# When the turned y is moved, cast and multiplied: the loads of the MLP's input in two chunks of a mixer kernel, and a third tile of w1's products ahead

## The chip, the cores and the metric

The kernel runs on one core of one Trainium2 chip. The metric is the device time of one execution in microseconds (us); the median of several executions is what is compared. A difference of about 0.3% can be told from no change.

## The reference, cut to what matters

One sequence of S = 2048 tokens of width D = 512. Two branches read the same layer-normalised input and their results are multiplied:

```python
xn = layernorm(x)
s = attention(xn, wqkv, wo)      # 32 heads of 16, causal, window of 256 tokens
y = layernorm(xn)
h = gelu(y @ w1 + b1)            # 512 -> 1792
g = silu(h @ w2 + b2)            # 1792 -> 512
out = x + s * g
```

All is float32. The kernel makes a float32 product from three products of two halves: a high part, which is a cast to the matmul's type fp32r, and a low part, which is the value less its high part (`PASSES`).

## The kernel before, in words

**Stages.** First x is normalised and turned. Then comes attention, written as 128 steps, t = 0 to 127 (`end = 16 * NQ`), from 16 starting steps on: each step has the scores and softmax of one block of 128 keys for four heads (`prob_block`, step t), the row maxima of a block 12 steps ahead (`max_block`, m = t + 12), the products with v (`pv_step`), and fills. Fills are matmuls of other work that keep TensorE (PE) busy: the projections of q and k of later heads and of v, and, from step 99 on, the first products with w1 of the first chunk of 512 tokens (`pair_h`). `tandem(t0, t1, one, two)` spreads a pair of such jobs over the slots of steps t0 to t1 and copies the two banks `fb` out at t1. `at(t, ...)` puts an operation into the middle of step t, `behind(t, ...)` at its end.

After attention follow the chunks of 512 tokens, one after another. The loop `for c in range(2)` does the first (c = 0) and the second (c = 1). In its step i it applies the gelu to tile `order[i]` of the 14 tiles of hidden features (`activate`: gelu and cast `gh` on ScalarE, the low part `gl` on VectorE), multiplies tile `order[i - 1]` with w2 (`project`, 12 matmuls), and makes the products of tile `order[i + 2]` with w1 (`hidden`, 12 matmuls) unless attention made them already. `end_chunk` adds b2, applies the silu, multiplies the attention output with wo (banks `s`, two at a time) and gates (`gated<-s,gated` on VectorE). Chunks 2 and 3 are done together afterwards with combined operands; their inputs (`first_y`, `second_y`, `combine_w`) are prepared in the steps of c = 1.

**What y is and how it is turned.** w1's products need y with features on the partitions, so y must be turned. Two ways are used. For the first chunk 16 PE transposes through the banks `fb` do it (`y_turn`, in steps 91 and 92 of attention). For the others VectorE turns 32 x 32 blocks in place (`turn_y`), the tile is written to DRAM (`z_d`), and four transfers for each group of 128 features fetch it in the turned order in pieces of 128 bytes (`fetch_y`, 16 transfers a chunk). `settle_y` then makes the high part (cast on ScalarE) and the low part (subtraction on VectorE) of one such group. The steps of the layer norm itself are the list `mlp["ln"]`, run piecewise by `y_steps(a, b)`: four statistics, one inversion, one shift, four normalisations.

**Where the second chunk's y stands before.** In c = 0: loaded at i = 4, statistics at i = 6 and 7, normalised at i = 10 and 11, turned at i = 11 and 12, fetched at i = 13 (all 16 transfers). It is settled inside `end_chunk(0)`, by `between(0)` and `between(2)`, ahead of the gating of the same places.

**What sets the order.** Each engine works its instructions in the order in which the program has them. SyncE (SP), which issues all transfers, keeps program order until the end of attention; behind that, its order is the one that the scheduler gives. PSUM pools hold the banks: in the chunk stage `ps_st` has two banks (w1's products and `s`), `ps_yt` two, which nothing uses until chunks 2 and 3, and `ps_mx` the accumulators `acc`.

Of the kernel before, what the change touches and what calls it, by code (L numbers as in the profile page):

```python
# [18 lines left out]
P = 128  # L19
# [31 lines left out]
def mixer_kernel(ctx, tc, x, wqk, wv, wo, w1, b1, w2, b2, out):  # L51
# [311 lines left out]
    def pair_qk(n, c):  # L363
# [11 lines left out]
        def finish(ps, t, copy):  # L375
# [383 lines left out]
    at(99, open_w1)  # L759
    for f, t in ((6, 91), (7, 91), (8, 92), (9, 94), (10, 94), (11, 99), (12, 99), (13, 101), (2, 101), (3, 103), (0, 103),  # L760
                 (1, 105), (4, 105), (5, 107)):
        at(t, fetch, "w1", f)
    for f, t, lo_at, lo_by in ((6, 94, 95, nc.vector), (7, 95, 97, on_pool), (8, 96, 98, on_pool), (9, 97, 99, nc.vector),
                               (10, 100, 102, nc.vector), (11, 102, 103, nc.vector), (12, 103, 105, on_pool),
                               (13, 105, 106, on_pool), (2, 106, 108, nc.vector), (3, 107, 109, on_pool),
                               (0, 108, 110, on_pool), (1, 109, 112, nc.vector), (4, 111, 113, on_pool),
                               (5, 112, 114, on_pool)):
        at(t, settle, "w1", f, nc.scalar.copy)
        at(lo_at, settle, "w1", f, None, lo_by)
# [101 lines left out]

    for g in range(4):
        fetch("wo", g)

    def load_y(c):
# [3 lines left out]

    def turn_y(c, i):  # L880

        y = mlp["y"][i]
        nc.vector.transpose(y, y)
        nc.sync.dma_start(z_d[c, i], y)

    def fetch_y(c, kt, dst):

        for k in range(4):
            at = z_d[c, 0, 0, 128 * kt + 32 * k: 128 * kt + 32 * k + 32]
            nc.sync.dma_start(dst[32 * k: 32 * k + 32].rearrange("p (t j) -> p t j", j=32),  # L890
                              bass.AP(tensor=at.tensor, offset=at.offset, ap=[[512, 32], [32 * 512, 16], [1, 32]]))

    def settle_y(kt):

        hi, lo = mlp["yy"][0][kt], mlp["yy"][1][kt]
        split(hi, lo, lo.bitcast(F32))

# [159 lines left out]
    def steps2(i):  # L1057

        if i in (-1, 1, 5, 6):
            mlp["ln"] = layernorm(mlp["y"], f"C{2 + (i > 1)}_{i}", True)  # L1060
            y_steps(0, 2 if i < 0 else 5)
        if i == 0:
            y_steps(2, 5)

    gated = None
    for c in range(2):
# [18 lines left out]
        order = [2, 3, 0, 1, 4, 5, *range(6, NF)] if c == 0 else [*range(NF)]  # L1085
        if c:
            hidden(0)
            hidden(1)
        o_from, o_late = (0, 0) if c else (8, 1)
        for i in range(NF + 1):  # L1090
            if i < NF:
                activate(order[i])
            if c and i in (1, 2, 6, 7):
# [11 lines left out]
            if i >= 1:  # L1105
                project(accs, [(order[i - 1], gs.pop(order[i - 1]))], order[0], order[-1])
            if i + 2 < NF and order[i + 2] not in made and order[i + 2] > 1:
                hidden(order[i + 2])
            if c == 0:
                if i == 2:  # L1110
                    den = fetch_sums()
                if 4 <= i < 8:
                    nc.vector.reciprocal(den[:, P * (i - 4): P * (i - 3)], den[:, P * (i - 4): P * (i - 3)])
                    if i == 7:
                        nc.sync.dma_start(rden_d.rearrange("g a (c t) -> (g a c) t", c=NCH), den)
                if i == 4:
                    mlp["y"] = load_y(1)
                if i == 6:
                    mlp["ln"] = layernorm(mlp["y"], "C1", False)
                for back, (a, b) in enumerate(((0, 2), (2, 4), (4, 5), (5, 6), (6, 8), (8, 10))):  # L1120
                    if i == 6 + min(back, 5):
                        y_steps(a, b)
                if i in (11, 12):
                    turn_y(1, 2 * i - 22)
                    turn_y(1, 2 * i - 21)
                if i == 13:
                    for kt in range(KT):
                        fetch_y(1, kt, mlp["yy"][1][kt].bitcast(F32))
                    mlp["y"] = load_y(2)
            else:  # L1130
                steps2(i)
                if i == 3:
                    for k in range(4):
                        turn_y(2, k)
                if i == 4:
                    kept[0] = gated[:, 2:4]
                    kept[1] = bigp.tile([P, 2, 512], F32, tag="wb1", name="y2_21")
                    for kt in range(KT):
                        fetch_y(2, kt, kept[kt // 2][:, kt % 2])
                    mlp["y"] = load_y(3)  # L1140
                if i in (5, 6):
                    first_y(2 * i - 10)
                    first_y(2 * i - 9)
# [15 lines left out]
            if 0 <= k < 4:  # L1159
                wanted.append(load_o(c, k))  # L1160
            if c and i in (0, 1, 5, 6):
                y_steps(5, 6)
# [161 lines left out]
```

## Time and profile before

| | |
|---|---|
| median of 3 runs | 758.77 us (757.1 to 759.68) |
| the profiled execution's own time | 758.06 us |
| its span, first to last instruction | 756.3 us |
| PE busy | 732.9 us (97%) |
| VectorE (DVE) busy | 517.6 us (68%) |
| ScalarE (ACT) busy | 438.4 us (58%) |
| GpSimd (POOL) busy | 298.7 us (39%) |
| DMA packets | 84025, of them 36640 under 512 bytes |

Times are counted from the span's start. Attention's steps end at about 431 us, c = 0 runs to about 495 us, c = 1 to about 587 us, chunks 2 and 3 to the end. PE matmuls overlap each other, so that the step between their starts is shorter than one's duration. In a row of the timeline, what stands in brackets is the engine's idle time before the row, and what ended it. All of the kernel's instructions are recorded under one helper's line (L43), so rows are told apart by the names of the tiles: `xnT`, `yh` are areas that hold y's halves in the chunk stage, `w` and `wos` hold w2's and wo's, `or` and `ohl` are the attention output before and behind its split, `w<-rden_d` brings in the reciprocals of the softmax sums.

### The profile page before, as it was taken

Reading aid. Unit: us, or ns where it says so; the run is one execution under the profiler, and the core shown is the slowest. Engines: PE = TensorE matmul, PEld = TensorE weight load, DVE = VectorE, ACT = ScalarE, POOL = GpSimd, SP = SyncE. Lnnn points to the kernel's source line nnn. Section 1 sums busy time; section 2 is a strip of 40 time slices with the busy share of each in tenths; the row PEclk is TensorE's granted clock in tenths of the full one; section 3 lists DMA queues with packets and bytes.
Section 4 is the critical chain, followed back from the end, with each engine's and each line's share of the span. In section 5 each row is a group of like instructions: output and inputs, shape, how many; then the busy total and the mean of one; then the engine's idle time right before and its main releaser. Section 6 shows DMA issues by size and latency. Waiting matters only on the chain.

```text
span 756.3 us, 18805 instructions
## 1 busy us (share of the span) xinstructions
PE 732.9 (97%) x7360; PEld 587.3 (78%) x7360; DVE 517.6 (68%) x793; ACT 438.4 (58%) x740; POOL 298.7 (39%) x644
## 2 busy tenths in 40 slices
PE   8999999999999999999999999799999999999997
PEld 7886777777778887776776787588778888888886
DVE  7886777877766779887873458656558765676643
ACT  7757767867676676788867645244534643442001
POOL 7414767766666555859776400030101100001102
PEclk9999999999999999999999999899999999999999
DMA  8633346766655544646634474857253232244621
GB/s 292 183 77 81 87 120 160 215 160 164 162 137 137 144 120 127 169 119 178 196 107 135 144 251 129 202 158 183 53 139 98 98 107 72 73 161 131 204 61 56
DMA packets 84025, 105.71 MB, mean 140 GB/s; under 512 B 36640, under 2 KB 36896, under 8 KB 83936
## 3 DMA queue, kind: packets, MB, share of 16 engines
q1 hardware_dynamic: 83936, 104.50, 49.5%
q8 instruction: 58, 0.95, 0.5%
q14 instruction: 31, 0.25, 0.1%
HBM read 54.53 MB, written 32.77 MB: 115 GB/s over the span
## 4 chain that ended last, share of the span: by engine, by line
PE 80%; DVE 6%; ACT 5%; DMA 3%; issue 2%; POOL 1%; SPq 1%; DVEq 0%; ACTq 0%; POOLq 0%
PE fb L43 18%; PE acc L43 15%; PE zo L43 11%; PE p L43 9%; PE stb L43 9%; PE s L43 6%; PE xy L43 5%; PE h L43 4%; ACT pt L43 4%; PE pv L43 3%; SPq L43 1%; POOL pt L43 1%; DVE y L43 1%; DVE xy L43 1%; DMA w<-rden_d 1%
## 5 line engine op out<-in xcount | busy, mean ns | idle before, releaser
L43 POOL TENSOR_SCALAR_AFFINE_SELECT pt<-pt 128x256 f32<-128x256 f32 x480 | 192.9, 426 | 133.7 <-ACT pt L43 131.7
L43 ACT ACTIVATE pt<-stb 128x768 f32<-128x768 f32 (+1 forms) x244 | 188.5, 773 | 62.5 <-PE stb L43 55.0
L43 DVE TENSOR_REDUCE mt<-xy 128x4 f32<-128x1024 f32 (+1 forms) x128 | 152.6, 1192 | 4.4
L43 DVE COPY_PREDICATED xy<-upper,zo 128x512 f32<-128x512 int32 x112 | 77.8, 695 | 70.5 <-PE xy L43 62.9
L43 POOL TENSOR_TENSOR xo<-xo,gated 128x512 f32<-128x512 f32 x15 | 19.9, 1331 | 225.2 <-DVE gated L43 218.1
L43 PE MATMUL fb<-xnT,wqb 64*128 64x512 f32 (+1 forms) x684 | 104.6, 397 | 0.2
L43 PE MATMUL zo<-pt,vt 128*17 128x128 f32 x2880 | 103.8, 275 | 0.3 <-POOL pt L43 0.3
L43 PE MATMUL stb<-qk 64*128 64x384 f32 (+1 forms) x488 | 97.1, 393 | 6.1 <-ACT pt L43 3.9
L43 PE MATMUL acc<-w,gh 128*128 128x512 f32 x320 | 98.6, 389 | 0.0
L43 PEld LDWEIGHTS stb<-qk 64*128 64x128 f32 x488 | 45.9, 183 | 51.4 <-ACT pt L43 46.2
L43 PEld LDWEIGHTS zo<-pt,vt 128*17 128x17 f32 x2880 | 67.5, 97 | 15.6 <-issue 6.4
L43 PEld LDWEIGHTS fb<-xnT,wqb 64*128 64x128 f32 (+1 forms) x684 | 64.6, 185 | 11.0 <-DVE pjr L43 1.4
L43 PEld LDWEIGHTS acc<-w,gh 128*128 128x128 f32 x320 | 60.1, 188 | 12.4
L43 PE MATMUL acc<-w,gl 128*128 128x512 f32 x160 | 62.8, 392 | 0.9 <-DVE gl L43 0.9
L43 PE MATMUL xy<-qk 64*128 64x256 f32 (+2 forms) x536 | 58.4, 291 | 0.2 <-DVE mt L43 0.2
L43 PEld LDWEIGHTS xy<-qk 64*128 64x128 f32 x536 | 46.7, 185 | 6.7 <-issue 3.1
L43 PE MATMUL s<-wos,ohl 128*128 128x512 f32 (+1 forms) x204 | 47.2, 392 | 4.7 <-DVE gated L43 4.7
L43 ACT COPY oraw<-zo 128x128 f32<-128x128 f32 x128 | 34.0, 266 | 29.3 <-PE zo L43 28.8
L43 PEld LDWEIGHTS s<-wos,ohl 128*128 128x128 f32 x204 | 38.6, 198 | 12.8 <-DVE gated L43 5.1
L43 ACT ACTIVATE gated<-acc 128x512 f32<-128x512 f32 x16 | 8.7, 595 | 64.3 <-DVE acc L43 64.3
L43 PEld LDWEIGHTS zo<-qk 64*128 64x128 f32 x448 | 38.3, 185 | 4.6 <-issue 1.4
L43 ACT COPY p<-p 128x512 f32<-128x512 f32 x21 | 12.3, 585 | 47.4 <-PE p L43 40.1
(188 smaller groups left out, 1234.0 us busy)
## 6 DMA issues: line engine op xcount, KB each, us to landing
qk<-sh SPq DMA_DIRECT2D x128, 128.0 KB
qk<-pjr SPq DMA_DIRECT2D x64, 128.0 KB
oT_d<-oraw SPq DMA_DIRECT2D x32, 256.0 KB
w_d<-in_w_dram SPq DMA_DIRECT2D x14, 512.0 KB
x<-in_x_dram SPq DMA_DIRECT2D x16, 256.0 KB
or<-oT_d SPq DMA_DIRECT2D x16, 256.0 KB
w<-rden_d SPq DMA_DIRECT2D x16, 256.0 KB
xo<-in_x_dram SPq DMA_DIRECT2D x16, 256.0 KB
```

The costliest lines, as they stand in the source:

```text
L43: r = issue(*args, **kwargs)
```

## The change

It has five parts.

1. The first chunk's y is no longer turned by PE. VectorE turns it (at the ends of steps 83, 85, 86 and 87), four transfers write it and 16 fetch it, two in each of steps 88 to 95; it is settled in steps 93 to 100, half a group in each. The layer norm's pieces run one to two steps earlier. The fills of the last group of heads go over steps 85 to 91 and 92 to 98 (before 85 to 90 and 93 to 98), and w1's first tiles are fetched and split some steps later; one low part goes from GpSimd to VectorE.
2. The second chunk's y is loaded at the start of the chunk stage, ahead of wo, normalised in steps i = 2 to 6 of c = 0, and turned at i = 6 and 7. Its 16 fetches are spread over i = 8 to 13 and its casts over i = 11 to 14 of the loop; `between` no longer holds them.
3. wo is fetched at i = 2.
4. In c = 1, w1's products are made three tiles ahead instead of two; the odd tiles take the banks of `ps_yt`, so four banks are used.
5. What c = 1 does for chunks 2 and 3 (second layer norm of the last chunk, `first_y`, `second_y` and what follows them) stands one step later, with the first chunk-2 transfers over two steps.

```diff
-            free += 2 * (t == 90)
...
-    def y_turn(kt):
-        for i in range(4):
-            nc.tensor.transpose(fb[kt % 2][:, P * i: P * (i + 1)], mlp["y"][i][:, P * kt: P * (kt + 1)], ident)
-        split(mlp["yy"][0][kt], mlp["yy"][1][kt], fb[kt % 2])
+    def turn_y(c, i):
+        y = mlp["y"][i]
+        nc.vector.transpose(y, y)
+        return z_d[c, i], y
+
+    def fetch_y(c, kt, dst, groups=range(4)):
+        for k in groups:
+            at = z_d[c, 0, 0, 128 * kt + 32 * k: 128 * kt + 32 * k + 32]
+            nc.sync.dma_start(dst[32 * k: 32 * k + 32].rearrange("p (t j) -> p t j", j=32),
+                              bass.AP(tensor=at.tensor, offset=at.offset, ap=[[512, 32], [32 * 512, 16], [1, 32]]))
+
+    def settle_y(kt, part=None, src=None):
+        hi, lo = mlp["yy"][0][kt], mlp["yy"][1][kt]
+        halves(hi, lo, lo.bitcast(F32) if src is None else src, part)
...
-                               ((75, 79), (80, 84)), ((85, 90), (93, 98))), 2):
+                               ((75, 79), (80, 84)), ((85, 91), (92, 98))), 2):
...
-    for i, t in enumerate((77, 78, 81, 82, 83, 83, 85, 86, 87, 89)):
+    for i, t in enumerate((76, 77, 78, 81, 82, 82, 83, 85, 86, 87)):
         at(t, y_steps, i, i + 1)
+        if i >= 6:
+            at(t, lambda i=i, t=t: behind(t, nc.sync.dma_start, *turn_y(0, i - 6)))
     at(88, open_yy)
-    for kt in range(KT):
-        fills.setdefault((91 + kt // 2, kt % 2), []).append((y_turn, (kt,)))
+    for m in range(4 * KT):
+        at(88 + m // 2, lambda kt=m // 4, k=m % 4: fetch_y(0, kt, mlp["y"][kt], (k,)))
+    for kt, t in enumerate((93, 95, 98, 99)):
+        for part in range(2):
+            at(t + part, lambda kt=kt, part=part: settle_y(kt, part, mlp["y"][kt]))
...
-    for f, t in ((6, 91), (7, 91), (8, 92), (9, 94), (10, 94), ...
+    for f, t in ((6, 93), (7, 94), (8, 96), (9, 96), (10, 97), ...
...
-    for g in range(4):
-        fetch("wo", g)
...
+    mlp["y"] = load_y(1)
...
-        if i in (-1, 1, 5, 6):
+        if i in (-1, 1, 6, 7):
             mlp["ln"] = layernorm(mlp["y"], f"C{2 + (i > 1)}_{i}", True)
...
-            hs[f] = ps_st.tile([P, 512], F32, tag="b", name=f"h_{c}_{f}")
+            hs[f] = (ps_yt if c and f % 2 else ps_st).tile([P, 512], F32, tag="b", name=f"h_{c}_{f}")
...
-        if c:
-            hidden(0)
-            hidden(1)
+        ahead = 2 + c
+        for f in range(ahead if c else 0):
+            hidden(f)
...
-            if c and i in (10, 12):
+            if c and i in (11, 13):
                 rest[0]()
-            if c and i in (10, 13):
+            if c and i in (11, 13):
                 rest[1]()
...
-            if i + 2 < NF and order[i + 2] not in made and order[i + 2] > 1:
-                hidden(order[i + 2])
+            if i + ahead < NF and order[i + ahead] not in made and order[i + ahead] > 1:
+                hidden(order[i + ahead])
...
-                if i == 4:
-                    mlp["y"] = load_y(1)
-                if i == 6:
+                if i == 2:
+                    for g in range(4):
+                        fetch("wo", g)
                     mlp["ln"] = layernorm(mlp["y"], "C1", False)
-                for back, (a, b) in enumerate(((0, 2), (2, 4), (4, 5), (5, 6), (6, 8), (8, 10))):
-                    if i == 6 + min(back, 5):
-                        y_steps(a, b)
-                if i in (11, 12):
-                    turn_y(1, 2 * i - 22)
-                    turn_y(1, 2 * i - 21)
-                if i == 13:
-                    for kt in range(KT):
-                        fetch_y(1, kt, mlp["yy"][1][kt].bitcast(F32))
+                if 2 <= i < 7:
+                    y_steps(2 * i - 4, 2 * i - 2)
+                if i in (6, 7):
+                    for k in (2 * i - 12, 2 * i - 11):
+                        nc.sync.dma_start(*turn_y(1, k))
+                for m in range(max(0, 3 * i - 25), min(16, 3 * i - 22)) if i >= 8 else ():
+                    fetch_y(1, m // 4, mlp["yy"][1][m // 4].bitcast(F32), (m % 4,))
+                if i >= 11:
+                    settle_y(i - 11)
+                if i == 14:
                     mlp["y"] = load_y(2)
...
-                if i == 8:
+                if i == 9:
                     for k in range(4):
-                        turn_y(3, k)
+                        nc.sync.dma_start(*turn_y(3, k))
                     fetch_second(0)
-                if i in (9, 11):
-                    rest = second_y(i // 11)
-                if i == 10:
+                if i in (10, 12):
+                    rest = second_y(i // 12)
+                if i == 11:
                     fetch_second(1)
...
         def between(i):
-            if c == 0 and i in (0, 2):
-                settle_y(i)
-                settle_y(i + 1)
```

More of the change, by code (lines that the diff above doesn't have):

```diff
@@ L759, in mixer_kernel @@
     at(99, open_w1)
-    for f, t in ((6, 91), (7, 91), (8, 92), (9, 94), (10, 94), (11, 99), (12, 99), (13, 101), (2, 101), (3, 103), (0, 103),
+    for f, t in ((6, 93), (7, 94), (8, 96), (9, 96), (10, 97), (11, 99), (12, 99), (13, 101), (2, 101), (3, 103), (0, 103),
                  (1, 105), (4, 105), (5, 107)):
         at(t, fetch, "w1", f)
-    for f, t, lo_at, lo_by in ((6, 94, 95, nc.vector), (7, 95, 97, on_pool), (8, 96, 98, on_pool), (9, 97, 99, nc.vector),
-                               (10, 100, 102, nc.vector), (11, 102, 103, nc.vector), (12, 103, 105, on_pool),
+    for f, t, lo_at, lo_by in ((6, 96, 97, nc.vector), (7, 97, 98, nc.vector), (8, 100, 102, on_pool), (9, 101, 104, nc.vector),
+                               (10, 104, 106, nc.vector), (11, 102, 103, nc.vector), (12, 103, 105, on_pool),
                                (13, 105, 106, on_pool), (2, 106, 108, nc.vector), (3, 107, 109, on_pool),
@@ L878, in load_y @@
         return [load(mlp["yp"], "y", xn_d[4 * c + i], f"y_{c}_{i}") for i in range(4)]
[L880 to L896, printed above, removed]
+    mlp["y"] = load_y(1)
     def fetch_sums():
@@ L1092, in mixer_kernel @@
                 activate(order[i])
-            if c and i in (1, 2, 6, 7):
+            if c and i in (1, 2, 7, 8):
                 y_steps(6, 10)
-            if c and i in (10, 12):
+            if c and i in (11, 13):
                 rest[0]()
-            if c and i in (10, 13):
+            if c and i in (11, 13):
                 rest[1]()
@@ L1133, in mixer_kernel @@
                     for k in range(4):
-                        turn_y(2, k)
+                        nc.sync.dma_start(*turn_y(2, k))
                 if i == 4:
@@ L1137, in mixer_kernel @@
                     kept[1] = bigp.tile([P, 2, 512], F32, tag="wb1", name="y2_21")
-                    for kt in range(KT):
+                if i in (4, 5):
+                    for kt in (2 * i - 8, 2 * i - 7):
                         fetch_y(2, kt, kept[kt // 2][:, kt % 2])
+                if i == 5:
                     mlp["y"] = load_y(3)
-                if i in (5, 6):
-                    first_y(2 * i - 10)
-                    first_y(2 * i - 9)
-                if i == 8:
+                for kt in {6: (0, 1), 7: (2,), 8: (3,)}.get(i, ()):
+                    first_y(kt)
+                if i == 9:
                     for k in range(4):
-                        turn_y(3, k)
+                        nc.sync.dma_start(*turn_y(3, k))
                     fetch_second(0)
-                if i in (9, 11):
-                    rest = second_y(i // 11)
-                if i == 10:
+                if i in (10, 12):
+                    rest = second_y(i // 12)
+                if i == 11:
                     fetch_second(1)
@@ L1160, in mixer_kernel @@
                 wanted.append(load_o(c, k))
-            if c and i in (0, 1, 5, 6):
+            if c and i in (0, 1, 6, 7):
                 y_steps(5, 6)
```

## The prediction, made before the changed kernel was run

> **What bounds the kernel now.** I read the page first, for the engine that fills the span.
>
> ```profile
> span 756.3 us, 18805 instructions
> ...
> PE 732.9 (97%) x7360; PEld 587.3 (78%) x7360; DVE 517.6 (68%) x793; ACT 438.4 (58%) x740; POOL 298.7 (39%) x644
> ```
>
> PE leaves 23.4 us of the span. A change pays if it takes work off PE, fills its gaps, or keeps its clock up. So I next asked for windows by stage (columns: length, then busy time of PE, PEld, DVE, ACT, POOL, then granted clock, DMA share, GB/s), and for what PE waited for in the chunk stage.
>
> ```profile
> 432.20:477.20 45.00, 44.11 (x193) 35.63 (x192) 31.35 (x56) 22.88 (x37) 1.39 (x1) 1.00 0.58 193
> 477.20:495.70 18.50, 13.79 (x50) 10.87 (x49) 7.87 (x12) 5.93 (x9) 2.41 (x2) 0.82 0.88 218
> 495.70:580.80 85.10, 81.86 (x359) 66.88 (x358) 53.43 (x106) 40.07 (x63) 8.00 (x7) 1.00 0.46 119
> ```
> ```profile
> PE s L43 <- DVE gated L43: 4.7, 1, 4.7
> PE h L43 <- ACT g L43: 3.2, 2, 1.8
> PE acc L43 <- DVE gl L43: 0.9, 2, 0.5
> ```
>
> The middle window, the end of the first chunk, is the only one in which PE both waits long and runs at a clock below 1. The timeline there shows the chain.
>
> ```profile
> 471.41 1.30 DVE L43 STREAM_TRANSPOSE y<-y 128x512 f32<-128x512 f32 x2
> ...
> 475.94 0.86 SPq L43 DMA_DIRECT2D z_d<-y  x2
> ...
> 477.40 5.60 PE L43 MATMUL s<-wos,ohl 128*128 128x512 f32 x24
> ...
> 479.89 8.78 SPq L43 DMA_DIRECT2D xnT<-z_d  x16
> ...
> 483.97 0.62 ACT L43 CAST yh<-xnT 128x512 fp32r<-128x512 f32 x1 [2.37 <-DMA xnT<-z_d]
> 484.62 0.69 DVE L43 TENSOR_TENSOR xnT<-xnT,yh 128x512 fp32r<-128x512 f32 x1 [4.14 <-ACT yh L43]
> ...
> 486.97 1.28 DVE L43 TENSOR_TENSOR gated<-s,gated 128x512 f32<-128x512 f32 x2
> 487.71 8.34 PE L43 MATMUL s<-wos,ohl 128*128 128x512 f32 x24 [4.71 <-DVE gated L43]
> ...
> 495.88 0.39 PE L43 MATMUL h<-yh,xnT 128*128 128x512 f32 x1
> ```
>
> The second chunk's y is turned late, written at 475.94 and fetched from 479.89. VectorE's queue has the low halves of that y ahead of the gating, so the gating of the first `s` bank, whose matmuls had long ended, waits for a transfer; `s` has two banks, so PE stands for 4.71 us. Then 24 matmuls take 8.34 us where the same 24 took 5.60. That 2.74 us is the clock's, by the 0.82 of the window. The gap and its echo cost 7.45 us.
>
> The Trainium skill (TensorE: Matmul & The Clock Gate, part 1 on the clock gate) says that about 3.4 us without work drop PE to half clock until it has been busy for as long. The 4.71 us gap and the window's 0.82 agree.
>
> **The change part by part: the end of the first chunk.** y goes through the same stations five steps earlier, and its casts stand inside the loop. The 4.71, the 2.74 and the two stalls on `gl` (0.9, which the turning at i = 11 and 12 caused) go: 8.35 us. What is late next? PE works one `project` in 12 x 44.11 / 193 = 2.74 us, and VectorE now has more than that in i = 5 to 7.
>
> ```profile
> 450.38 0.94 DVE L43 RECIPROCAL den<-den 128x128 f32<-128x128 f32 x1
> ...
> 463.59 1.00 DVE L43 TENSOR_SCALAR y<-y,mvC,rsC 128x512 f32<-128x512 f32 x2
> ```
>
> With 0.69 for a low half (row 484.62), i = 5 has `gl`, a low half of w2, a reciprocal and two normalisations: 3.32 us. i = 6 has two turns (1.30, row 471.41) on top, 4.62; i = 7 the same without normalisations, 3.62. The excess over 2.74 is 0.58 + 1.88 + 0.88 = 3.34 us. `gh` has two buffers, so `gl` of a tile can start only when PE begins the tile before it, and it is needed at the third matmul of its own, 2 x 0.23 = 0.46 us in: of 2.74 + 0.46, the cast takes 0.62 and the low half 0.69, which leaves 1.9 us of slack. So PE loses 3.34 - 1.9 = 1.4 us (none if VectorE enters i = 5 early, 2.4 if it enters a microsecond late, since y's load now precedes the sums' on SP). Queued behind this on VectorE is the reciprocal whose write SP needs before `w<-rden_d`, and SP now has the fetches between those loads: eight fetches at 8.78 / 16 = 0.55 us stand ahead of the third. The product with `or` waits, and `gl` behind it: I take 0.9 us, with bounds 0 and 1.5. The last cast comes about a microsecond before the gating needs VectorE, so I expect no hole. Net: -8.35 + 1.4 + 0.9 = -6.05 us, between -8.35 and -4.45. wo's later fetch is hidden: it takes the place that y's load had on SP, and wo's first split was and stays at i = 6.
>
> **Attention.** PE loses 16 transposes; VectorE gets four turns and SP 20 transfers.
>
> ```profile
> L43 DVE STREAM_TRANSPOSE y<-y x12: 668/670/708, 468.0 to 549.4; 128x512 f32<-128x512 f32 x12
> ```
> ```profile
> 326.93 0.45 PE L43 MATMUL stb<-qk 64*128 64x384 f32 x2 [0.17 <-ACT pt L43]
> 327.31 0.66 PE L43 MATMUL fb<-ident,y 128*128 128x128 f32 x4
> 327.89 0.44 PE L43 MATMUL zo<-qk 64*128 64x128 f32 x4
> ...
> 346.30 0.45 PE L43 MATMUL stb<-qk 64*128 64x384 f32 x2 [0.39 <-ACT pt L43]
> ```
> ```profile
> 313.07 1.23 DVE L43 TENSOR_REDUCE mt<-xy 128x4 f32<-128x1024 f32 x1
> 314.21 0.71 DVE L43 TENSOR_SCALAR y<-y,mvC,rsC 128x512 f32<-128x512 f32 x1
> 315.01 0.70 DVE L43 COPY_PREDICATED xy<-upper,zo 128x512 f32<-128x512 int32 x1
> ...
> 317.81 0.70 DVE L43 COPY_PREDICATED xy<-upper,zo 128x512 f32<-128x512 int32 x1 [0.39 <-PE xy L43]
> ```
> ```profile
> 318.05 2.47 SPq L43 DMA_DIRECT2D qk<-sh  x4
> ...
> 342.10 0.56 SPq L43 DMA_DIRECT2D qk<-mT_d  x1
> ```
>
> Four transposes take 327.89 - 327.31 = 0.58 us of PE, 16 take 2.3; with the 0.17 stall, -2.5. The fills stay the same in number.
>
> VectorE was nearly full there: steps 86 to 87 take 2.80 us (315.01 to 317.81), of which 0.39 idle. Steps 85, 86 and 87 now each get a turn of 0.67 while each keeps a normalisation. PE has one pair of `xy` banks, so its next maxima wait for the reduction: 3 x (0.67 - 0.39) = 0.84 us, a little more for the turn of step 83: +1.2, between 0 and 2.0. Behind them on VectorE stand only the masks and reductions that this already counts. The casts and low halves are as many as before, on steps that `y_turn` has left.
>
> SP waits for the fourth turned tile, written at the end of step 87, to land (at most 3.1 us by rows 475.94 and 479.89, 476.80 to 479.89; I take 2), and q and k rows, row maxima (`qk<-mT_d`) and w1 queue behind. Sixteen fetches at 0.55 and four writes at 0.43 (row 475.94, two in 0.86) are 10.5 us over steps 88 to 95, where its row of `qk<-sh` alone takes 0.62 each. Counting SP's order from step 88 on at these prices, the row-maxima load that before issued at 342.10, 4.2 us ahead of step 98 (346.30) which reads it, would issue at about 344.8 and land two later, at 346.8, with PE there at 346.3 - 1.3 = 345.0: a wait of some +1.8 us, between 0 and 3. Sum for attention: -2.5 + 1.2 + 1.8 = +0.5, between -2.5 and +2.5.
>
> The Trainium skill (DMA: Bandwidth & Descriptors, "Specifications") asks for pieces of 512 bytes or more; the new fetches have 128. Its rule speaks against this part. The window 477.2 to 495.7, with 16 such fetches, shows a DMA share of 0.88 at 218 GB/s.
>
> **The second chunk's loop.** Four banks take PE's wait for `g` away, in principle 3.2 us.
>
> ```profile
> 541.24 0.50 PE L43 MATMUL h<-yh,xnT 128*128 128x512 f32 x1 [1.41 <-ACT g L43]
> ...
> 565.13 0.50 PE L43 MATMUL h<-yh,xnT 128*128 128x512 f32 x1 [1.83 <-ACT g L43]
> ...
> 576.14 6.06 PE L43 MATMUL s<-wos,ohl 128*128 128x512 f32 x26
> ```
> ```profile
> 547.59 2.48 DVE L43 STREAM_TRANSPOSE y<-y 128x512 f32<-128x512 f32 x4
> ...
> 556.05 0.69 DVE L43 TENSOR_TENSOR gated<-y,gated 128x512 f32<-128x512 f32 x1 [5.40 <-DMA y<-z_d]
> ...
> 571.38 0.69 DVE L43 TENSOR_TENSOR gl<-g,gh 128x512 fp32r<-128x512 f32 x1 [1.19 <-ACT gh L43]
> ...
> 577.42 2.76 DVE L43 TENSOR_TENSOR acc<-acc,b2s 128x512 f32<-128x512 f32 x4
> 580.09 0.68 DVE L43 TENSOR_TENSOR gated<-s,gated 128x512 f32<-128x512 f32 x1
> ```
>
> But VectorE's chain, from turning the last chunk's y (547.59) through the fetch to b2's additions (577.42), is 29.83 us long and ends just in time: the first gating ends at 580.77, and PE wants the bank at 576.14 + 5.60 = 581.74. Measured from the first `h` (495.88, call it S), the turning stood at S + 51.7 and the third `s` at S + 85.9. After, the turning stands at i = 9, behind `gl` of that step, whose `gh` needs PE past `project(7)`: four products ahead, then seven pairs and one, 19 x 2.74 = 52.1 behind S, and 1.6 for cast (0.62), low half (0.69) and some waiting: S + 53.7, two later than before. The chain sheds one `gl` (0.69) and the 1.19 wait on `gh`, 27.9. So b2's additions start at S + 81.6, and the third `s` at S + 81.6 + 2.76 + 0.68 = S + 85.0. PE, which gets there at about S + 83, waits again, for another reason. Net -0.8 us, between -3.2 (no wait) and +1.9 (chain not shortened).
>
> **Sum.** -6.05 + 0.5 - 0.8 = -6.35. Against the profiled execution's 758.06 us (1.8 around its span of 756.3): 751.7 us. That execution is 0.7 below the median of 758.77 and inside the runs' spread, so I leave it.
>
> **The rivals.**
>
> A, *the banks and the lighter attention pay in full*: VectorE's chain in the tail finds the transfers earlier, or attention has the slack that I deny it. With -2.4 more in the second loop, or -2.5 in attention: about 749.2. For it: both new waits are worked out to a microsecond only. Against: VectorE at 53.43 of 85.10 is not the average that counts; the chain is serial.
>
> B, *SP falls behind in attention* (the side of slower). If none of SP's 10.5 us finds free time in steps 88 to 95, q, k and row maxima come 10.5 late, less 2 of slack: PE stands 8.5 us and loses the clock as behind the gap at 487.71, 2.74. -6.35 - 1.8 + 8.5 + 2.74 = +3.1: 761.2. It decides from a lag of about 8 us on. Against: loads run several steps ahead.
>
> C, *a gap in the second loop's tail drops the clock*. Gaps of 1.41 and 1.83 left it at 1.00, the 4.71 one did not; I expect about 2 there, in two parts. If they join to over 3.4 us, 2.74 more: 754.4. That 3.4 is the clock-gate page's; the rows alone put the point between 1.83 and 4.71.
>
> D, *the hole stays*: the last cast comes after the point where the first gating is due, as before, and VectorE is blocked. Then 4.71 + 2.74 stay, 0.9 goes, 2.3 comes: 758.06 + 1.4 + 0.5 - 0.8 = 759.2. The cast would have to be more than 6 us later than worked out.
>
> **How the numbers follow.** Forecast 0.50, A 0.25, C 0.12, D 0.07, B 0.06. The forecast's own terms reach from about 746 to 757 with their bounds partly adding up; A and C lie within it. The range 746.0 to 756.5 leaves out D, B and the outer tails. 0.3% of 758.77, about what a measurement of this kernel can tell from no change, is 2.3 us: faster means under 756.5. Forecast, A and C less their tails give 0.83; D and the upper tail 0.11; B 0.06.
>
> **What would show it.** Right: no PE wait for `gated` near 480, granted clock 1.00 there, the first `h` of the second chunk about 18.5 - 6 us after the first `s`; short waits of `acc` on `gl` at i = 7 or 8 and near i = 13; PE waiting for `gated` or `gl` at the end of the second loop instead of for `g`; in steps 86 to 98, waits of PE on `mt` or a transfer into `qk`. Wrong: waits over 3 us anywhere before the third chunk, a window with a clock under 1, or an attention stage that is longer by more than 2.5 us.

## The result, and the profile after

The change makes the kernel slower: 770.97 us (770.56 to 772.18) against 758.52 us (757.10 to 759.68), ratio 1.0168 with a 95% interval of 1.0146 to 1.0189. The prediction had said 751.7, between 746.0 and 756.5. The profiled execution after has 770.56 us, and 768.8 between its first and last instruction.

The page of the changed kernel: PE is busy for about as long as before in a longer span, and its clock falls once, a little under half way.

```profile
span 768.8 us, 18798 instructions
...
PE 736.0 (96%) x7344; PEld 585.4 (76%) x7344; DVE 523.5 (68%) x798; ACT 437.9 (57%) x740; POOL 299.1 (39%) x643
...
PEclk9999999999999999996999999999999999999999
```

Four marks on PE's timeline split the span: an `xy` product of attention ahead of which no edit acts, the start of `acc<-w,g_first`, where attention's products are done, the first `h` of the second chunk, and the end. The first mark, in the trace of before:

```profile
285.82 0.40 PE L43 MATMUL xy<-qk 64*128 64x256 f32 x4
```

| stretch | before | after | difference | predicted |
|---|---|---|---|---|
| start to `xy` | 285.82 | 286.14 | +0.3 | 0 |
| `xy` to `g_first` | 146.36 | 159.41 | +13.05 | +0.5 |
| `g_first` to the second chunk's first `h` | 63.70 | 63.14 | -0.56 | -6.05 |
| from there to the end of the span | 260.4 | 260.1 | -0.3 | -0.8 |

So the loss is attention's, and the first chunk brings almost nothing. PE's timeline after (start, length, instruction, and in brackets the idle time before it and what ended it):

```profile
286.14 0.41 PE L43 MATMUL xy<-qk 64*128 64x256 f32 x4
...
348.81 0.69 PE L43 MATMUL stb<-qk 64*128 64x384 f32 x2 [3.66 <-ACT pt L43]
...
356.90 0.69 PE L43 MATMUL stb<-qk 64*128 64x384 f32 x2 [4.50 <-DMA qk<-mT_d]
...
445.55 5.60 PE L43 MATMUL acc<-w,g_first 128*128 128x512 f32 x24
...
488.31 0.50 PE L43 MATMUL acc<-w,gl 128*128 128x512 f32 x1 [0.98 <-DVE gl L43]
...
492.28 0.50 PE L43 MATMUL acc<-w,gl 128*128 128x512 f32 x1 [0.95 <-DVE gl L43]
...
494.68 1.52 PE L43 MATMUL s<-wos,ohl 128*128 128x512 f32 x6
496.84 1.23 PE L43 MATMUL s<-wos,ohl 128*128 128x512 f32 x3 [0.65 <-DVE ohl L43]
499.11 9.74 PE L43 MATMUL s<-wos,ohl 128*128 128x512 f32 x39 [1.04 <-DVE ohl L43]
508.69 0.39 PE L43 MATMUL h<-yh,xnT 128*128 128x512 f32 x1
```

Two gaps close to each other in attention, of 3.66 and 4.50 us, and the clock with them, in windows of 10 us after (length, busy time of PE, PEld, DVE, ACT, POOL, then the granted clock); the last row is the end of the first chunk:

```profile
340.00:350.00 10.00, 6.12 (x90) 4.66 (x88) 4.99 (x7) 4.22 (x9) 3.51 (x9) 0.87 0.66 139
350.00:360.00 10.00, 5.50 (x42) 4.32 (x44) 4.38 (x6) 3.43 (x7) 2.31 (x6) 0.50 0.74 206
360.00:370.00 10.00, 9.02 (x140) 6.29 (x135) 8.59 (x12) 8.69 (x16) 6.95 (x16) 0.94 0.61 169
...
494.68:508.69 14.01, 12.31 (x49) 8.70 (x48) 8.53 (x14) 5.99 (x8) 3.83 (x3) 1.00 0.75 248
```

PE's busy time there, times the share of the clock that it lacked, is 6.12 x 0.13 + 5.50 x 0.50 + 9.02 x 0.06, about 4.1 us. The two gaps are 8.2 us. Together they are 12.3 of the 13.05.

Both gaps come from SP's queue. SP after, in those steps:

```profile
333.80 3.90 SPq L43 DMA_DIRECT2D y<-z_d  x4
...
338.40 3.65 SPq L43 DMA_DIRECT2D qk<-sh  x4
...
344.65 0.43 SPq L43 DMA_DIRECT2D xnT<-w_d  x1
...
348.34 0.71 SPq L43 DMA_DIRECT2D qk<-qk  x1
349.16 4.26 SPq L43 DMA_DIRECT2D qk<-sh  x4
353.52 1.18 SPq L43 DMA_DIRECT2D qk<-pjr  x2
354.74 0.55 SPq L43 DMA_DIRECT2D qk<-mT_d  x1
```

and SP before, in the same steps, with the one long entry of its waits between 318 and 356:

```profile
325.82 1.64 SPq L43 DMA_DIRECT2D xnT<-w_d  x3
333.12 0.53 SPq L43 DMA_DIRECT2D mT_d<-mT  x1
...
334.97 3.89 SPq L43 DMA_DIRECT2D qk<-sh  x4
...
342.70 0.57 SPq L43 DMA_DIRECT2D qk<-qk  x1
343.37 2.48 SPq L43 DMA_DIRECT2D qk<-sh  x4
```
```profile
SPq L43 <- DVE mT L43: 5.6, 1, 5.6
```

Before, SP had one free stretch of 5.6 us there. After, it is gone: the load of the row maxima (`qk<-mT_d`) issues at 354.74, 12.64 us later than the 342.10 of before, and PE stands for it up to 356.90. Mainly two things stand ahead of that load that did not before. One is 14 of the 16 fetches, 9.52 us by their rows. The other is q and k rows of the next pair, from 348.34 to 354.70 (0.71 + 4.26 + 1.18 = 6.15 us): before, these rows went out behind the load, from 342.70 on, and the fills' other steps have put them ahead of it (from the end of step 95 to that of step 94, where the load stands). The first gap is the same delay by another way. The load of a tile of w1 (`xnT<-w_d`) goes out at 344.65, its cast waits at the head of ScalarE's queue, and the exponential that PE needs stands behind that cast. ScalarE's waits after, between 330 and 372:

```profile
ACT xnT L43 <- DMA xnT<-w_d: 7.5, 2, 3.8
```

In the end of the first chunk, what was forecast did happen: no wait for `gated` is left near 480 and the clock is 1.00. In its place stands a row of short waits for `gl`, `gh` and `ohl`. SP, ScalarE and VectorE after:

```profile
478.01 6.83 SPq L43 DMA_DIRECT2D xnT<-z_d  x8
484.89 0.59 SPq L43 DMA_DIRECT2D or<-oT_d  x1
485.52 0.58 SPq L43 DMA_DIRECT2D w<-rden_d  x1
...
490.42 3.93 SPq L43 DMA_DIRECT2D xnT<-z_d  x5
```
```profile
484.64 0.63 ACT L43 CAST yh<-xnT 128x512 fp32r<-128x512 f32 x1 [3.59 <-DMA xnT<-z_d]
...
495.10 0.62 ACT L43 CAST xnT<-xnT 128x512 fp32r<-128x512 f32 x1 [6.54 <-DMA xnT<-z_d]
```
```profile
481.81 0.69 DVE L43 TENSOR_TENSOR or<-or,w 128x512 f32<-128x512 f32 x1 [2.77 <-DMA w<-rden_d]
...
490.93 0.69 DVE L43 TENSOR_TENSOR or<-or,w 128x512 f32<-128x512 f32 x1 [1.00 <-DMA w<-rden_d]
```

Eight fetches take 6.83 us and stand ahead of the loads of the softmax sums; the product `or<-or,w` waits on VectorE with `gl` behind it, and the cast waits on ScalarE with the next gelu behind it. The new loop position put the casts in the way of what PE needs at once.

### The profile page after: what moved, and what is told of

Its sections match the earlier page's. It is cut to its first block, busy times and chain, and to the rows that moved or that the text cites. A ratio compares the mean times of both kernels' runs of the same rounds, so it can differ in the third digit from the quotient of the medians.

```text
span 768.8 us, 18798 instructions
## 1 busy us (share of the span) xinstructions
PE 736.0 (96%) x7344; PEld 585.4 (76%) x7344; DVE 523.5 (68%) x798; ACT 437.9 (57%) x740; POOL 299.1 (39%) x643
## 4 chain that ended last, share of the span: by engine, by line
PE 68%; DVE 9%; DMA 8%; ACT 6%; issue 4%; POOL 2%; SPq 2%; DVEq 0%; ACTq 0%; POOLq 0%
PE fb L43 16%; PE acc L43 11%; PE zo L43 10%; PE p L43 9%; PE stb L43 8%; PE s L43 5%; PE xy L43 4%; ACT pt L43 4%; PE pv L43 3%; PE h L43 3%; DMA oT_d<-oraw 2%; SPq L43 2%; DMA y<-z_d 1%; POOL pt L43 1%; DVE xy L43 1%
## 5 line engine op out<-in xcount | busy, mean ns | idle before, releaser
L43 PE MATMUL fb<-xnT,wqb 64*128 64x512 f32 (+1 forms) x684 | 106.5, 402 | 0.3
L43 PEld LDWEIGHTS s<-wos,ohl 128*128 128x128 f32 x204 | 36.3, 188 | 13.1 <-DVE ohl L43 3.3
L43 PE MATMUL zo<-qk 64*128 64x128 f32 x448 | 40.0, 255 | 1.0 <-DVE xy L43 0.7
```

The source lines that it names most:

```text
L43: r = issue(*args, **kwargs)
```

## The experiments

The table has all runs; "attention" is the stretch from the `xy` mark to `g_first`, "to h" the one behind it, each from that run's trace. The kernels that leave attention as it was (e1, e7, e8, e11, e12, e15) give 146.11 to 146.40 for the former, so that a few tenths are no difference there. Runs without an interval are single executions. Each ratio is to runs of the kernel before that were taken along with that kernel (their medians are 757.5 to 758.5).

| run | time | ratio to before, 95% | attention | to h |
|---|---|---|---|---|
| before | 758.5 | | 146.36 | 63.70 |
| after | 770.97 | 1.0168 (1.0146 to 1.0189) | 159.41 | 63.14 |
| e1 parts 2 to 5 | 759.0 | 1.0026 (1.0013 to 1.0038) | 146.11 | 65.48 |
| e2 part 1 | 771.4 | | 159.19 | 64.80 |
| e3 part 1, no fetches | 762.14 | | 148.53 | 65.05 |
| e4 part 1, fetches by ScalarE | 766.07 | | 156.13 | 62.19 |
| e5 part 1, 512-byte transfers | 770.53 | | 156.53 | 65.62 |
| e6 part 1, w1's loads ahead | 771.41 | | 158.83 | 64.42 |
| e7 banks, and PE turns | 752.12 | 0.9917 (0.9886 to 0.9948) | 146.30 | 56.44 |
| e8 parts 2 to 5, no fetches | 752.44 | | 146.30 | 57.88 |
| e9 part 1, no turns or fetches | 760.06 | | 147.89 | 63.95 |
| e10 before, 16 transfers more | 761.26 | | 149.79 | 62.90 |
| e11 parts 4 and 5 | 757.87 | 0.9994 (0.9985 to 1.0004) | 146.38 | 64.08 |
| e12 before, PE turns | 752.55 | 0.9929 (0.9912 to 0.9947) | 146.40 | 56.42 |
| e13 before, fills moved | 760.88 | | 149.67 | 63.26 |
| e14 before, w1 later | 760.02 | | 147.70 | 64.03 |
| e15 e1, casts behind the loop | 757.67 | | 146.31 | 63.92 |

### Which part loses: e1 and e2

e1 keeps `y_turn` and the steps of before in attention and has parts 2 to 5; e2 has part 1 alone.

> The kernel before with parts 2 to 5 of the change (second chunk's y early, casts in the loop, three tiles ahead in four banks), and the first chunk's y still turned by PE in steps 91 and 92. Theory S (SyncE's queue in attention makes all the loss): attention ends where it did, the first g_first product at 432.2 us, and the rest is as in the changed kernel, so the whole comes to 758.5 - 0.6 - 0.3, about 757.5 us. Rival: part of the loss comes from the chunk stage itself (its order of transfers): then over 760 us.

> The kernel before with part 1 alone (first chunk's y turned by VectorE and fetched by 16 transfers in attention). Theory S: all of the 13.4 us later end of attention is here, the first g_first product near 445.5 us and the whole about 771.5 us; PE waits 4 us each for ACT pt and for qk<-mT_d between 340 and 360 us. Rival (the parts only hurt together): under 765 us.

e2 shows the whole of attention's loss, with the same two waits (3.67 at 348.05, 4.51 at 356.14). e1, at 759.0, lies between its two forecasts, and is slightly slower than before, not faster: attention is untouched, and the first chunk's end is 1.8 us longer, in one wait that the changed kernel does not have in this size. PE's timeline of e1:

```profile
480.85 0.50 PE L43 MATMUL acc<-w,gl 128*128 128x512 f32 x1 [3.21 <-DVE gl L43]
```

So part 1 costs attention 12.8 us, and parts 2 to 5 bring nothing as they stand.

### What of part 1: e3, e9, e5, e10

e3 leaves the 16 fetches out of e2, so that y holds the blocks in the wrong places; e9 leaves out VectorE's turns and the writes too.

```diff
-        at(88 + m // 2, lambda kt=m // 4, k=m % 4: fetch_y(0, kt, mlp["y"][kt], (k,)))
+        pass
```

> As e2, but the 16 fetches of the first chunk's turned y are left out: the turns and the four writes stay, and the halves are cast from the tile as it stands, so the first chunk's values are not those of the reference. Theory S: without the fetches SyncE keeps up, PE's waits over 1 us between 330 and 365 us go, and the first g_first product comes at 430.5 to 432 us (16 transposes less, VectorE's turns more). Rival V (VectorE's turns and the moved fills make the loss): it stays over 440 us.

> Part 1 alone without the fetches (as the run that cost 2.9 us more than expected), and now without VectorE's four turns and the four writes as well; the values are not the reference's. Theory 1 (the turns delay the masks, the writes hold SP): the first product behind attention comes at about 431.5 us or earlier, 3 to 4 us before the 435.06 of the run with the turns. Theory 2 (the fills spread over other steps and w1's later loads cost it): it stays within 1 us of 435.06.

The fetches cost 159.19 - 148.53 = 10.7 us, the clock's fall among it, which goes with them. The turns and writes cost 148.53 - 147.89 = 0.6. What is left, 147.89 - 146.36 = 1.5 although PE has 16 transposes fewer, is below (e13, e14). e3 missed its forecast of 430.5 to 432 by 3 us, and e9 says that neither the turns nor the writes are the cause. PE still waits for the load of the row maxima, in e3 and, below it, in e9:

```profile
347.65 0.44 PE L43 MATMUL stb<-qk 64*128 64x384 f32 x2 [1.28 <-DMA qk<-mT_d]
```
```profile
346.46 0.44 PE L43 MATMUL stb<-qk 64*128 64x384 f32 x2 [1.51 <-DMA qk<-mT_d]
```

This is not for want of room: in e9 SP itself stands for 4.5 us there, waiting for `sh`. But the q and k rows stand ahead of the load in both kernels, as in the changed one (e9 has four `qk<-sh` at 337.94, 3.84 us, and the load at 344.04).

Do the fetches cost as bytes in small pieces or as places in SP's queue? e5 puts 16 transfers of 512 bytes between DRAM tensors in the fetches' places, which nothing waits for. e10 puts the same 16 into the kernel before, and nothing else.

```diff
-        at(88 + m // 2, lambda kt=m // 4, k=m % 4: fetch_y(0, kt, mlp["y"][kt], (k,)))
+        at(88 + m // 2, lambda m=m: nc.sync.dma_start(tiny_d[m: m + 1], x[m: m + 1, 0:128]))
```

> As e3 (turns and writes of the first chunk's y, no fetches, so its values are not the reference's), but in the places of the 16 fetches SyncE issues 16 transfers of 512 bytes, DRAM to DRAM, that nothing waits for. e3's attention ended at 435.1 us, e2's, with the fetches, at 444.8. Theory S1 (the issue slots on SyncE are what costs): 16 x 0.55 = 9 us of SyncE come back, and the end moves to 441 us or later. Rival S2 (the 128-byte pieces cost: they slow the landing of everything behind them, and SyncE's issues with it): it stays within 2 us of e3, under 437 us.

> The kernel before, with 16 transfers of 512 bytes from DRAM to DRAM issued by SP, two in each of steps 88 to 95; nothing uses what they write. Theory (SP's issue slots in these steps are the scarce thing, whatever else part 1 does): attention ends 4 to 8 us later than 432.18, with a PE wait for qk<-mT_d or ACT pt near 350. Rival (before has room for 16 slots, and only together with part 1's other moves do they cost): later by under 2 us.

Places in the queue. e5 loses 156.53 - 148.53 = 8.0 of the 10.7 us with next to no bytes; two rows of its SP timeline and two of PE's:

```profile
330.99 2.67 SPq L43 DMA_DIRECT2D tiny_d<-in_x_dram  x4
...
351.11 0.56 SPq L43 DMA_DIRECT2D qk<-mT_d  x1
```
```profile
345.72 0.69 PE L43 MATMUL stb<-qk 64*128 64x384 f32 x2 [2.48 <-ACT pt L43]
353.39 0.69 PE L43 MATMUL stb<-qk 64*128 64x384 f32 x2 [4.08 <-DMA qk<-mT_d]
```

Four such issues take 2.67 us, 0.67 each. In the prediction the Trainium skill's rule of 512-byte pieces (DMA: Bandwidth & Descriptors, "Specifications") stood against this part. These runs leave it at most the 2.7 us between e5 and e2, in which SP's wait for the fourth turned tile to land is contained as well (2.7 us in the changed kernel, none in e5); the rest comes without any 128-byte piece. e10 costs 3.4 us (4.1 by the bare mark at 436.27, the lower end of what was expected), over the rival's 2: the kernel before has 5.6 us of room, the 16 issues take 10.05 us, and PE pays for part of the rest, the fall of the clock included. Its PE timeline and windows:

```profile
348.82 0.44 PE L43 MATMUL stb<-qk 64*128 64x384 f32 x2 [2.23 <-ACT pt L43]
```
```profile
345.00:348.80 3.80, 1.58 (x22) 1.05 (x19) 1.76 (x2) 1.80 (x4) 2.46 (x5) 1.00 0.48 144
348.80:352.00 3.20, 3.18 (x34) 2.39 (x34) 2.37 (x3) 2.23 (x4) 2.53 (x5) 0.62 0.61 128
```

So the same 16 places cost 3.4 us in the kernel before and 8.0 beside the rest of part 1. The rival of e10 was right in this much: more than half of the cost arises only together with the other moves. The two queues differ in the order told above. In e10 the load of the row maxima goes out at 345.68, ahead of the next q and k rows, and PE does not wait for it; in e5 it goes out at 351.11, behind them, and PE stands for 4.08 us. No run has the fetches with the fills left as they were, so how much of the loss is due to that order is not measured by itself.

### Can the places be moved: e4 and e6

e4 lets ScalarE issue the fetches, at steps 91 to 94; e6 loads w1's tiles 6 to 8 ahead of them.

```diff
+        at(91 + m // 4, lambda kt=m // 4, k=m % 4: fetch_y(0, kt, mlp["y"][kt], (k,), nc.scalar))
```

> As e2, but the 16 fetches are issued by ScalarE, four in each of steps 91 to 94, instead of by SyncE. The same bytes in the same 128-byte pieces go over the same DMA engines. Theory S: SyncE's other transfers go out on time, so PE waits for no qk<-mT_d and w1's loads are there; the end of attention comes back by at least 6 of the 13.4 us, less what ScalarE loses by issuing. Rival D (the small pieces fill the DMA engines, whoever issues them): q, k and w1 land as late as in e2 and the end of attention stays within 3 us of e2's.

> As e2 (part 1 alone), but the loads of w1's tiles 6, 7 and 8 stand at step 92, ahead of that step's fetches of y, instead of at steps 93, 94 and 96. Only SyncE's order changes. In e2 ScalarE stood up to 3.8 us before the casts of these tiles, with the exponentials of attention behind them, and PE waited 3.67 us for ACT pt. Theory (ScalarE's queue passes SyncE's delay on): that wait goes or falls under 1.5 us, the wait for qk<-mT_d stays or grows to 5 to 6 us, and the end of attention comes 2 to 6 us earlier than e2's 444.8. Rival (the waits are one delay, whatever is late first): the end stays within 1.5 us of 444.8.

e4 came back by 3.1 us only, at the rival's bound: it takes the load off SP, whose late `qk<-mT_d` costs PE 1.17 there, and puts it on ScalarE, whose four rows of four issues took 1.98, 2.62, 2.46 and 2.67 us, and PE waited 9.2 us for `pt` instead. The Trainium skill (DMA: Bandwidth & Descriptors, "Issuing engines are not separate DMA queues") says that issuing from several engines saves only the sequencer's time, which is usually small beside the transfer. Here it is not small on either engine: the rows of e4's issues on ScalarE add up to 9.73 us. e6 gained nothing: the wait for `pt` became 1.43, the wait for `qk<-mT_d` 8.53. For w1's loads it is one delay, and their place only decides where it shows.

### The rest of part 1: e13 and e14

e13 moves only the last group's fills to steps 85 to 91 and 92 to 98 (`y_turn` then writes into banks `fb` that the fills use, so that the projections of that group are not the reference's, and three short waits on `fb` come in, 1.4 us); e14 only w1's first loads and splits to the steps of the change.

```diff
-            free += 2 * (t == 90)
...
-                               ((75, 79), (80, 84)), ((85, 90), (93, 98))), 2):
+                               ((75, 79), (80, 84)), ((85, 91), (92, 98))), 2):
```

> The kernel before, with only the last group's fills over steps 85 to 91 and 92 to 98. Theory 1 (the fills' other steps delay the q and k loads on SP, whose row of shifts then issues later): attention ends 1.5 to 3 us later than 432.18, with a PE wait for a transfer into qk near 346. Theory 2 (w1's later loads hold ScalarE): within 0.7 us of 432.18.

> The kernel before, with only w1's first tiles loaded and split at the later steps of the change. Theory 1 (the fills' other steps cost it): attention ends within 0.7 us of 432.18. Theory 2 (w1's casts, then in the steps of the exponentials with the full load, hold ScalarE): 1.5 to 3 us later, with PE waits for ACT pt.

Neither theory holds alone. e14 costs attention 1.3 us, with no wait over 0.5. e13 costs 3.3, with a wait of 0.84 for `qk<-mT_d` at 349.13, whose load goes out at 346.70 behind the q and k rows; 1.4 of the 3.3 belongs to its own clash on `fb`, which leaves 1.9. What has to be accounted for is 1.5 + 2.3 = 3.8, since e9 also lacks the transposes: the two edits make 3.2 of it if their costs add up, which no run with both shows, and the rest stays open.

### The first chunk's end: e8, e15, e7, e11, e12

e8 leaves the 16 fetches of the second chunk's y out of e1, so that chunk's values are not the reference's. e15 keeps them and has all casts and low halves at i = 14.

> As e1 (parts 2 to 5), but the 16 fetches of the second chunk's turned y are left out; the halves are cast from what the area holds, so the second chunk's values are not the reference's. In e1 PE lost in c = 0 what the hole had cost, in waits for gl, gh and ohl. Theory (the fetches and the loads of the softmax sums share SyncE and the DMA engines, and the casts that wait for them stand in ScalarE's and VectorE's queues ahead of gh, gl and ohl): those waits fall from about 6 us to under 2.5, and the first h of the second chunk comes 4 us or more earlier than in e1, counted from the first g_first product. Rival (VectorE simply has too much work there): within 1.5 us of e1.

> Parts 2 to 5 with the first chunk's y as before (the run that took 65.5 us from g_first to the second chunk's first h), and the four groups of casts and low halves all at i = 14 instead of one in each of i = 11 to 14. Theory (casts that wait for a fetch hold gelu and gh behind them in ScalarE's queue): about 3 us of the gl waits go, 61 to 63 us from g_first to the first h. Rival (the loads of the softmax sums behind the fetches on SP are what is late): within 1 us of 65.5.

Without the fetches the stretch falls from 65.48 to 57.88. With the casts out of the loop it falls only to 63.92: the waits for `ohl` go, and one long wait stays, for the softmax sums behind the fetches on SP; behind it the clock is 0.50 for 4.4 us (480.40 to 484.80). PE and VectorE of e15:

```profile
480.40 0.79 PE L43 MATMUL acc<-w,gl 128*128 128x512 f32 x1 [4.73 <-DVE gl L43]
```
```profile
479.05 0.69 DVE L43 TENSOR_TENSOR or<-or,w 128x512 f32<-128x512 f32 x1 [5.93 <-DMA w<-rden_d]
```

That lies between the two forecasts: the casts were in the way, and behind them the sums are late all the same. What is shown to cost is the 16 fetches, 7.6 us by e8; no run here tells their places on SP from their bytes, as e5 does for attention.

e7, e11 and e12 take the banks and the transposition apart. e11 has parts 4 and 5 on the kernel before; e12 gives the second chunk's y to PE, whose banks `ps_yt` are idle there; e7 has both.

```diff
-                if i in (11, 12):
-                    turn_y(1, 2 * i - 22)
-                    turn_y(1, 2 * i - 21)
+                if i in (12, 13):
+                    for kt in (2 * i - 24, 2 * i - 23):
+                        bank = ps_yt.tile([P, 512], F32, tag="b", name=f"yt_{kt}")
+                        for k in range(4):
+                            nc.tensor.transpose(bank[:, P * k: P * (k + 1)], mlp["y"][k][:, P * kt: P * (kt + 1)], ident)
+                        split(mlp["yy"][0][kt], mlp["yy"][1][kt], bank)
...
-                    for kt in range(KT):
-                        fetch_y(1, kt, mlp["yy"][1][kt].bitcast(F32))
...
-            if c == 0 and i in (0, 2):
-                settle_y(i)
-                settle_y(i + 1)
```

> The kernel before with parts 4 and 5 (three tiles ahead in four banks), and with the second chunk's y turned by PE: 16 transposes into the two spare banks in i = 12 and 13 of c = 0, split from there by ScalarE and VectorE, no write to DRAM and no fetches for that chunk, nothing to settle in end_chunk(0). Theory: the hole of 4.71 us, its 2.74 us of clock and the 0.9 us on gl go, the transposes cost 2.4 us, the second loop gains about 1: 757.5 - 5.95 - 1 = about 750.5 us. Rival: the casts and low halves of i = 12 and 13 push gl and the split of or late, and PE waits there for 3 us or more: 753 us or over.

> Parts 4 and 5 alone (three tiles ahead in four banks, and the preparation of chunks 2 and 3 one step later); the first chunk and the second chunk's y as before. Theory (the forecast's step: the waits for g go, the tail's chain on VectorE takes most of it back): 0.3 to 0.8 us faster than before, within what can be told. Rival (the banks pay in full): 2.5 to 3.2 us faster.

> The kernel before, with only the second chunk's y turned by 16 PE transposes in i = 12 and 13 of the first chunk's loop, in place of VectorE's turns, the writes and the 16 fetches; two tiles ahead in two banks as before. Theory (the gain of the version with both is the hole and the clock drop that go): 752.5 to 753.5, within 1.3 us of the version with the four banks. Rival (the banks carry part of that gain): 754.5 or more.

e11 cannot be told from before: PE's waits for `g` are gone, and one of 1.7 for `gated` and one of 0.5 for `gh` stand in their place. e12 gains 0.7% with a few lines, and e7's interval contains e12's value, as e12's theory had it. e7's own 752.12 lies between its two forecasts (about 750.5, and 753 or over). PE's timeline of e12:

```profile
470.68 1.03 PE L43 MATMUL yt<-ident,y 128*128 128x128 f32 x8
474.30 1.03 PE L43 MATMUL yt<-ident,y 128*128 128x128 f32 x8
477.94 11.04 PE L43 MATMUL s<-wos,ohl 128*128 128x512 f32 x48
```

The 16 transposes take 2.06 us of PE. The hole, the fall of the clock and the two waits for `gl` go with the fetches and VectorE's turns: 48 products run through in 11.04 us, and the stretch is 56.42 instead of 63.70. Both e7 and e12 beat the kernel before and the changed one; the change went the other way, from PE to VectorE and SP.

## Why the prediction was wrong, point by point

**Attention (+0.5 predicted, between -2.5 and +2.5; +13.05 measured).** The step that failed is SP's term, +1.8 between 0 and 3. It had the right mechanism, place and victim: `qk<-mT_d` late, PE waiting for it at step 98. The issue was put at 344.8; it came at 354.74. Three things were wrong in it. First, SP's order: the prediction took the fills as "the same in number" and gave their move no price, but it puts 6.15 us of q and k rows ahead of the load. Second, the price and the free time: the 14 fetches ahead of the load took 0.68 us each, not 0.55, 1.8 us more in all; the 0.55 came from a stretch in which SP did little else, and the four of `qk<-sh` at 334.97, in 3.89 us against the 2.47 of those at 318.05, could have warned of it. Of the room that had to take this up, the view of SP's waits has 5.6 us in one piece, against the 10.5 us that the prediction itself had counted, and in the changed kernel SP again stands for 2.7 us of that stretch, until the fourth turned tile has landed. Third, the loads of w1 were named as queued behind, but not their casts at the head of ScalarE's queue. Of the signs that were to show the prediction wrong, all came: waits over 3 us, a clock under 1, and attention longer by more than 2.5 us. Rival B was what happened in attention, at 0.06, and even its price was low: 8.5 us of standing against 8.16 measured in two gaps, but 2.74 for the clock against about 4.1, because the second gap came while the clock was still down (0.50 in the 3.59 us between the two). Its 761.2 falls short of 770.97 for another reason too: it kept the gain in the first chunk.

**VectorE's turns (+1.2 predicted).** Somewhat high: e3 less e9 is 0.6 with the four writes, and PE's waits for `xy` after are 0.7 in all.

**The transposes (-2.5).** They go, but attention is 1.5 us longer without them even where turns, writes and fetches are left out (e9). The moved fills and w1's later loads, which the prediction had priced at nothing, make 3.2 us of that difference of 3.8 if their costs add up (e13, e14).

**The end of the first chunk (-6.05 predicted, -0.56 measured).** The hole and the clock's fall went, as predicted; rival D did not come. VectorE's excess in i = 5 to 7 was 1.4 predicted and 0.54 + 0.18 = 0.7 measured; another 0.38 came earlier, at 463.00, behind the statistics of a y that VectorE got only at 457.26. The term that failed is the waits behind SP's loads (`or` and `gl`): 0.9, at most 1.5, predicted. Measured, for `gh`, `gl` and `ohl` together, are 0.59 + 0.98 + 0.95 + 0.65 + 1.04 = 4.2 us of listed waits. The page counts a wait from the modelled end of the matmul before; from start to start, at the usual 0.23, the same five places and the 39 products behind them lose about 6 us. The eight fetches were taken at 8.78 / 16 each, 4.4 us; they took 6.83. And the casts inside the loop were seen only as safe for the gating, not as a wait in ScalarE's queue ahead of gelu and `gh`: e15 shows what they add, 1.6 us net of the clock that it loses.

**The second loop (-0.8 predicted, -0.3 measured).** Right within what can be told, and for the reason given: the waits for `g` went and PE waits for `gated` instead, 1.7 us, with the third `s` at 593.38, 84.7 behind the first `h` (85.0 predicted). e11, by itself, is 0.3 us faster than its runs of before, with an interval that contains no change, which agrees with it.

The range was too narrow because both SP terms had been bounded with a price from a quieter stretch, and because the terms did not hold what the moved fills do to SP's order.

## What to carry to other kernels

Before an operation goes from a busy engine to transfers, count the issues as an engine's work: add up the queue's free time from its own waits in exactly those steps, price an issue from a row taken where the queue is full, and compare. Then look whether anything else in the change puts other transfers ahead of the load that the bottleneck engine needs next. A cast that waits for a transfer belongs behind everything that the bottleneck engine needs next from the same queue. Where PE has idle PSUM banks, 2 us of transposes on PE can be cheaper than 16 transfers that cost no PE time at all.

## What the runs showed of the hardware that was not expected

An issue's price hardly depends on its size: the 16 of 512 bytes in e5 took 11.15 us by their rows, the 16 fetches of 64 KB in attention after 10.48.

The length of a gap does not by itself decide about the clock. In e7 a gap of 2.02 us was followed by a clock of 0.50, and in e10 one of 2.23 by 0.62, while in e1 the gap of 3.21 left it at 1.00. The gap on PE's timeline of e7, and the windows behind the gaps, of e7 and of e1:

```profile
561.97 0.73 PE L43 MATMUL acc<-w,gh 128*128 128x512 f32 x2 [2.02 <-ACT gh L43]
```
```profile
564.00:566.00 2.00, 2.00 (x6) 1.52 (x5) 2.00 (x4) 0.72 (x2) 0.00 (x0) 0.50 0.57 144
```
```profile
480.85:484.00 3.15, 3.15 (x14) 2.57 (x15) 0.00 (x0) 0.15 (x1) 0.00 (x0) 1.00 0.64 122
```

The Trainium skill (TensorE: Matmul & The Clock Gate, part 1) has the clock halved after about 3.4 us without work, in windows that run freely. These runs show a clock of 0.50 after a gap of 2.02 us and one of 1.00 after 3.21; the prediction's rival C, which set its point at 3.4, had no single point to set.
